# A step of 64 tokens of four batches instead of 128 tokens of two, in a kernel of linear attention followed by an MLP

## The chip, the cores and the metric

The kernel runs on one core of a Trainium2 chip. The metric is the time of one execution on the device in microseconds; before the change the median of three runs is 581.27 us (580.01 to 582.3). TensorE (PE) multiplies matrices, VectorE (DVE), ScalarE (ACT) and GpSimd (POOL) work on tiles, and SyncE (SP) issues most DMAs. Each engine works through its own queue in order and waits at semaphores.

## The reference

`r`, `k`, `v`, `w` have 4 batches, 8 heads, 768 tokens and 48 columns; `u` has one row for each head. A state of 48x48 for each batch and head decays by `w` from token to token. The result of the attention, 3072 tokens of 384 columns, goes through an MLP with 2048 hidden columns.

```
for t in range(S):
    cur = einsum('bhd,bhe->bhde', u[None] * kt, vt)
    y[:, :, t] = einsum('bhd,bhde->bhe', rt, state + cur)
    state = wt[:, :, :, None] * state + einsum('bhd,bhe->bhde', kt, vt)
x = y as (4*768, 384)
h = x @ w_in                          # 384 x 2048
g = h * erf(softplus(h))
out = g @ w_out                       # 2048 x 384
```

The two weights come as 64-bit floats, all else as 32-bit.

## The kernel before

The work is cut into 12 steps. A step takes 256 tokens: 128 tokens in a row (C) of each of two batches (NJ = 2); the two halves of 64 tokens (HC, NC = 2) are chunks that follow each other in time. Steps alternate between the two pairs of batches (`SPC` = 2), so that a pair's state passes from step s to step s + 2. Heads lie in pairs: e = 0 and 1 fill partitions 0 to 47 and 64 to 111, and JP = 8 counts batch times four pairs.

**Attention of a step.** Within a chunk the attention is made level by level: at level l TensorE multiplies left and right halves of blocks of 2^l tokens (`level_products`, L615), VectorE takes the wanted blocks into `own` (`take_level`, L633; the last level by ScalarE, L644) and scales r and k by products of decays (`scale`, L317). POOL makes these products (`totals`, L355, and L407). `from_own` (L650) multiplies `own` with v into `y`, in two halves with a `fence` (L666, a small VectorE copy) between. `through_state` (L673) adds r times the state: the state at the step's start `S` for the first chunk, `middle` for the second. `state_part` (L725) multiplies the transposed k with v for both chunks; from it come `middle` (faded start plus first part) and then `S_next` (faded `middle` plus second part): a POOL multiply into `faded`, a VectorE add, a POOL multiply, a VectorE add. After that y goes to `xT`. The last of the four groups of rows in y (`y3`) has to be shifted to other partitions: by small DMAs (L720), but in step 0 by three matmuls with a matrix of ones and zeros (`apart`, L700, in `hop`), which add into y before ScalarE copies it to xT.

**MLP.** `hidden` (L1064) multiplies xT with w_in (L1097, six matmuls for two of 16 columns of tiles, "a piece"), `project` and `project_fast` multiply with w_out (L1129, L1212). Pieces of the MLP of earlier steps stand in TensorE's queue between the levels of the present one, in an order written by hand (`place`, `beside`, `USUAL`, `LATE`). Steps 0 to 4 have a code path of their own (`attend_first`, `attend`); steps from 5 on go through `attend_late`, which makes the near levels on VectorE and POOL and takes k from a DRAM copy (`k_blocks`, `kT`, `spread_blocks`). The last two steps share their first product (`hidden_of_two`, L1300).

**Order.** The instructions of all five queues stand in the order in which the program calls them (`manual_schedule`).

**Weights.** In the first steps the 64-bit weights become 32-bit. `convert` (L222) has stages for each of 16 tiles: `l` loads the words by two DMAs of SP, behind a marker (a one-element copy, L241 or L243, that writes into the words' buffer and so makes the load wait for something), `b` scales the high words on ScalarE (L258), `r` the low words (L266), `h` shifts on VectorE (L275), `o` adds on POOL (L288). Three buffers hold words. In step 0, tiles 0 and 1 are loaded; the load of tile 2 stands behind the fence (L901), those of 3 and 4 behind the first copy into xT (L707), those of 5 and 6 behind the new state (L926). I call them load 2, load 3 and so on.

**Step 0** (`attend_first`, L819) has an inner loop over levels 2 to 5 with fillers on TensorE (`keep_busy`, a product with a zero state, L943; `stay_warm`, L934). After the last level come a filler, eight transposes of k (L889), the first `from_own`, `fence`, `state_part` of the first chunk, the second `from_own`, `middle`, `through_state` of the second chunk and `hop`. The second chunk's state part and the new state (`pending`, L921) wait for level 2 of step 1. Step 1 (`attend`, L948) puts `hop` in the middle of its level 1, and then a piece of step 0's MLP between its levels.

Of the kernel before, what the change touches and what calls it, by code (L numbers as in the profile page):

```python
# [61 lines left out]
def kernel(  # L62
# [21 lines left out]
    NB, n_pairs = out.shape[:2]  # L84
# [4 lines left out]
    SPC = NB // NJ  # L89
    assert C == P == NC * HC and HC == 1 << LOG and NE == 2 and D <= EP and NP * NE * D == DM == KT * P  # L90
    assert n_steps == SPC * n_pairs and NP == KT + 1 == 4 and NG == 2 and P // NEAR * NH == P
# [15 lines left out]

    states = [[const.tile([P, JP, D], FP32, name=f"s_{i}_{n}") for n in range(2)] for i in range(SPC)]
    middle = const.tile([P, JP, D], FP32, name="middle")
    faded = [const.tile([P, JP, D], FP32, name="faded")] * NC  # L110
# [111 lines left out]
    def convert(weights):  # L222
# [24 lines left out]
        def scale_high(i, part=slice(0, 2)):  # L247


            if i not in held:  # L250
                return
            if i < 2:
                base = ps_m.tile([P, NP * C], FP32, name="m")[:, :DM]
            else:
                base = y[:].rearrange("p e q j t -> p e (q j t)")[:, :, :DM]
            high = held[i]["words"][:, part, :, 1].bitcast(FP32)
            if i < signed:
                nc.scalar.activation(base, high, AF.Prelu, scale=2.0**-112, alpha=-(2.0**32))  # L258
            else:
                nc.scalar.mul(out=base, in_=high, mul=2.0**-112)  # L260
            held[i].setdefault("bases", []).append((base.bitcast(I32), part))
# [97 lines left out]
    def prepare(s):  # L359
# [63 lines left out]
        else:  # L423
            half = view(tots[NEAR_LOG + 1], 1, [[2, NC], [C >> NEAR_LOG + 1, JP]])
            quarter, last = (
                view(tots[NEAR_LOG], n, [[4, NC], [C >> NEAR_LOG, JP]]) for n in (1, 3)
            )
            to = over_blocks[:].rearrange("p (h b) n -> p b h n", h=NC)
            nc.gpsimd.tensor_mul(to[:, 0], quarter, half)
            nc.gpsimd.tensor_copy(out=to[:, 1], in_=half)  # L430
            nc.gpsimd.tensor_copy(out=to[:, 2], in_=last)
# [138 lines left out]
        if levels == NEAR_LOG:  # L570
            sum_up(NEAR_LOG, 0)
            sum_up(NEAR_LOG, 1)
            k_blocks = dram.tile([P, NEAR, D], FP32, name="k_blocks")
# [8 lines left out]
        if levels == NEAR_LOG:  # L582
# [16 lines left out]
    def parts_of(s):  # L599

        c, i = divmod(s, SPC)
        in_t, vt = loaded[s]
        made, tots, tot = ready[s]
        ends = tot.rearrange("p (n h) -> p n h", h=NC)
        return c, in_t, vt, made, states[i][c % 2], states[i][1 - c % 2], ends
# [67 lines left out]
    def through_state(s, xT):  # L673

        c, in_t, _, _, S, _, _ = parts_of(s)
        for h, state in enumerate((S, middle)):
            if not (c or h):
                continue
            t = slice(h * HC, (h + 1) * HC)
            for j, q in ((0, 2), (1, 2), (1, 0), (0, 0)) if not s else np.ndindex(NJ, NP // 2):  # L680
                q = q if not s else 2 * q
                for e in range(NE):
                    for p in (q + e, q + 1 - e):
# [3 lines left out]
                            lhsT=state[rows(e), n, :],  # L687
                            rhs=(in_t[:, 0, n] if s else first_pair(0, n))[rows(e), t],
# [7 lines left out]
        if not s:  # L696

            def hop():
                for kk in range(KT):
                    nc.tensor.matmul(  # L700
                        parts[kk], lhsT=apart[:, kk],
                        rhs=y3[:].rearrange("p (j t) -> p j t", j=NJ),
                        start=False, stop=True, skip_group_check=True,
                    )
                for kk in range(KT):
                    nc.scalar.copy(by_kk[kk], parts[kk])
                stages["l"](3, xT[:, KT - 1, 0:1], True)  # L707
                stages["l"](4)
                load_w(2)

# [14 lines left out]
    def state_part(s, kT, ps, halves=None):  # L725

        vt = loaded[s][1]
        if halves is None:
            halves = range(1 if s >= n_steps - SPC else NC)
        for n in range(JP):  # L730
            for h in halves:
                for e in range(NE):
                    t = slice(h * HC, (h + 1) * HC)
                    nc.tensor.matmul(  # L734
                        ps[h][e][rows(e), n, :D],
# [32 lines left out]
    def attend_late(s, run):  # L768

        c, in_t, vt, own, S, S_next, ends = parts_of(s)  # L770
# [10 lines left out]
        if before:  # L781
# [6 lines left out]
        nc.gpsimd.tensor_mul(faded[0][:], S[:], ends[:, :, 0:1].to_broadcast([P, JP, D]))  # L788
# [3 lines left out]
        kT = kTs[s]  # L792
        nc.vector.tensor_mul(
            kT[:].rearrange("p (e n) d -> p n e d", e=NE),
            kT[:].rearrange("p (e n) d -> p n e d", e=NE), spread[s][:],
        )
# [4 lines left out]
        if s + 1 < n_steps:  # L801
# [4 lines left out]
        ps = products([P, NC, JP, HC], 0)  # L806
        ps = [[ps[:, h]] * NE for h in range(NC)]
        state_part(s, kT, ps)
        run(2, following)
        nc.vector.tensor_add(middle[both], faded[0][both], ps[0][0][both, :, :D])  # L810
        run(3, following)
        if s < n_steps - SPC:
            nc.gpsimd.tensor_mul(
                faded[1][:], middle[:], ends[:, :, 1:2].to_broadcast([P, JP, D])
            )
            nc.vector.tensor_add(S_next[both], faded[1][both], ps[1][0][both, :, :D])
        run(4, following)

    def attend_first(xT):  # L819
# [5 lines left out]
        c, _, vt, made, S, S_next, ends = parts_of(0)  # L825
# [50 lines left out]
        for j, half in enumerate(halves):  # L876
            level_products(pp, first_pair, LOG, half)
            scale(0, LOG, batch=j)
        take_level(own, pp, LOG)

        kT = att.tile([P, NH, D], FP32, name="kT", bufs=1)
        kT_by_e = kT[:].rearrange("p (e n) d -> p e n d", e=NE)
        turned = [products([P, NE, JP, HC])]
        keep_busy(turned[0], (DM,))
        for j, half in enumerate(halves):
            if j:
                turned.append(products([P, NE, JP, HC]))
            for i, n in enumerate(half):
                nc.tensor.transpose(  # L889
                    turned[j][:, 0, 2 * i : 2 * i + 2], first_pair(1, n), ident[:]  # L890
                )
        from_own(0, own, 1)
        for half, ps, copy in zip(halves, turned, (nc.scalar.copy, nc.vector.tensor_copy)):
            copy(
                kT_by_e[:, :, half.start : half.stop],
                ps[:, 0].rearrange("p (n e) d -> p e n d", e=NE)[..., :D],
            )
        stages["b"](1, 0)
        stages["b"](1, 1)
# [3 lines left out]
        stages["h"](0)  # L903
        stages["h"](0)
        ps = [[products([P, NE, JP, HC], 1 - e)[:, e] for e in range(NE)]]
        state_part(0, kT, ps, (0,))
        from_own(0, own, 0)
        nc.scalar.copy(middle[rows(1)], ps[0][1][rows(1), :, :D])
        nc.vector.tensor_copy(middle[rows(0)], ps[0][0][rows(0), :, :D])
        stages["r"](1)  # L910
        stages["h"](1)
        stages["h"](1)
        wait_for(HC - 1)
        stages["o"](0)
        nc.gpsimd.tensor_mul(faded[1][:], middle[:], ends[:, :, 1:2].to_broadcast([P, JP, D]))
        totals(1)
        stages["o"](1)
        totals(*range(2, LOG + 1))
        through_state(0, xT)

        def pending():  # L921
            part = products([P, NE, JP, HC], turns["next"])[:, 0]
            state_part(0, kT, ps + [[part] * NE], (1,))
            nc.vector.tensor_add(S_next[both], faded[1][both], part[both, :, :D])
            load_third()
            stages["l"](5, S_next[:, 0, 0:1])  # L926

        turns["pending"] = pending
# [10 lines left out]
    def keep_busy(pp, columns=(DM, DM // 2)):  # L939

        zeros = states[1][0][:].rearrange("p n d -> p (n d)")
# [6 lines left out]
    def attend(s, xT, early, place, behind):  # L948

        c, in_t, vt, made, S, S_next, ends = parts_of(s)  # L950
# [718 lines left out]
```

## Time and profile before

| what | value |
|---|---|
| median of 3 runs | 581.27 us |
| profiled execution, its own time | 581.53 us |
| its span | 579.7 us |
| VectorE busy | 429.0 us |
| ScalarE busy | 354.8 us |
| POOL busy | 244.8 us |
| moved by DMA, mean over the span | 63.24 MB, 109 GB/s |
| of it, `w_in` words | 16 transfers of 384 KB, 5.3 us to landing |
| output tiles `o` | 23 transfers of 192 KB, two of 96 KB |
| a late step, from one L627 to the next | 281.87 to 326.17 us |

The profile is one execution seen by the hardware profiler; its times start at the span's start. A row of the timeline gives start and length, engine, line and operation, output and inputs, the number of instructions and, in brackets, how long the engine had been idle before and for what. TensorE shows two passes for each matmul of 32-bit numbers, so 16 matmuls are "x32". PEld is TensorE's loading of weights, PEclk its granted clock as a share of the full one. A line of the chain gives start, length and what ran.

### The profile page before, as it was taken

What the parts mean: (1) busy time and instruction counts of PE and PEld (TensorE: products, weight loads), DVE (VectorE), ACT (ScalarE), POOL (GpSimd) and SP (SyncE); (2) the same over time, 40 slices, a digit from 0 to 9 for tenths busy, and PEclk for the clock granted to TensorE, in tenths of its full rate; (3) what the DMA queues carried; (4) which work ended last, traced back from release to release, by engine and by line L of the source; (5) the groups of instructions that cost most, each with busy time, mean ns of one, the idle gap of its engine ahead of it and who ended that gap; (6) DMA issues with size and microseconds to landing.
All of it is one profiled execution on the core that took longest, in us unless ns stands there. A gap on an engine that the chain in (4) does not pass through costs nothing.

```text
span 579.7 us, 16499 instructions
## 1 busy us (share of the span) xinstructions
PE 572.8 (99%) x7240; PEld 492.2 (85%) x7240; DVE 429.0 (74%) x462; ACT 354.8 (61%) x478; POOL 244.8 (42%) x264
## 2 busy tenths in 40 slices
PE   8999999999999999999999999999999999999997
PEld 6678887688578668998998998898898899988997
DVE  7775876998894789699599599599599527256640
ACT  3658777545444698756766766766666661388700
POOL 3557391604793885284185175176174000000000
PEclk9999999999999999999999999999999999999999
DMA  7695662350453314245235236234232201000000
GB/s 261 190 325 233 235 207 83 148 161 2 145 151 98 107 44 169 41 139 177 41 125 192 39 124 193 39 111 163 47 110 83 47 8 37 1 1 2 28 27 28
DMA packets 54081, 63.24 MB, mean 109 GB/s; under 512 B 35160, under 2 KB 40568, under 8 KB 52984
## 3 DMA queue, kind: packets, MB, share of 16 engines
q1 hardware_dynamic: 53624, 61.98, 33.8%
q8 instruction: 57, 0.93, 0.7%
q10 hardware_dynamic: 384, 0.20, 0.1%
q14 instruction: 16, 0.13, 0.1%
HBM read 52.39 MB, written 8.69 MB: 105 GB/s over the span
## 4 chain that ended last, share of the span: by engine, by line
PE 95%; DVE 1%; POOL 1%; DMA 1%; issue 1%; ACT 0%; SPq 0%; DVEq 0%; POOLq 0%; ACTq 0%
PE m L1097 35%; PE m L1212 28%; PE m L1129 11%; PE pp L627 5%; PE pp L1300 4%; PE y L1300 2%; PE y L659 2%; PE y L685 2%; PE pp L734 2%; PE m L934 1%; DMA words<-in_moe_w_in 1%; PE pp L943 1%; PE pp L1010 1%; POOL tot_sb L355 0%; PE pp L1212 0%
## 5 line engine op out<-in xcount | busy, mean ns | idle before, releaser
L1097 PE MATMUL m<-xT,w_in_sb 128*128 128x256 f32 x960 | 214.8, 382 | 0.4 <-ACT h L1106 0.3
L1097 PEld LDWEIGHTS m<-xT,w_in_sb 128*128 128x128 f32 x960 | 180.1, 190 | 25.8 <-issue 0.5
L333 DVE TENSOR_TENSOR in<-in,tot_sb 128x1024 f32<-128x1024 f32 (+1 forms) x55 | 76.4, 1389 | 16.9 <-PE pp L627 15.5
L1106 ACT COPY h<-m 128x512 f32<-128x512 f32 x80 | 46.3, 579 | 59.7 <-PE m L1097 59.7
L1129 PE MATMUL m<-w_out_sb,h 128*128 128x384 f32 x192 | 64.3, 491 | 0.0
L1129 PEld LDWEIGHTS m<-w_out_sb,h 128*128 128x128 f32 x192 | 35.8, 190 | 23.4
L1212 PE MATMUL m<-mixed,h 128*128 128x192 f32 x256 | 45.6, 332 | 0.0
L1212 PE MATMUL m<-w_out_sb,h 128*128 128x192 f32 x256 | 44.8, 329 | 0.0
L1212 PEld LDWEIGHTS m<-mixed,h 128*128 128x128 f32 x256 | 41.4, 190 | 0.9
L1057 ACT ACT_TABLE_LOAD x30 | 38.5, 1283 | 5.9 <-DVE h L1062 5.4
L1212 PEld LDWEIGHTS m<-w_out_sb,h 128*128 128x128 f32 x256 | 41.6, 190 | 0.3
L1212 PE MATMUL m<-w_out_sb,room 128*128 128x192 f32 x240 | 41.5, 326 | 0.0
L1053 ACT ACT_TABLE_LOAD x30 | 38.5, 1283 | 3.2 <-issue 2.7
L462 POOL TENSOR_TENSOR words<-words,own 128x384 f32<-128x384 f32 x21 | 30.7, 1462 | 22.8 <-DVE words L493 13.1
L627 PEld LDWEIGHTS pp<-in 48*48 48x48 f32 (+4 forms) x2368 | 30.1, 120 | 11.8 <-issue 6.2
L503 POOL TENSOR_TENSOR words<-words 128x384 f32<-128x384 f32 x28 | 39.7, 1447 | 0.0
L1212 PEld LDWEIGHTS m<-w_out_sb,room 128*128 128x128 f32 x240 | 39.4, 190 | 0.0
L455 POOL TENSOR_TENSOR own<-rest 128x384 f32<-128x384 f32 x7 | 9.8, 1396 | 60.8 <-ACT o L1218 49.8
L627 PE MATMUL pp<-in 48*48 48x32 f32 (+4 forms) x2368 | 34.0, 206 | 0.2 <-DVE in L333 0.2
L503 POOL TENSOR_TENSOR rk<-words 128x384 f32<-128x384 f32 x28 | 32.4, 1186 | 0.0
L528 DVE TENSOR_REDUCE sums<-rk 128x16 f32<-128x768 f32 (+2 forms) x31 | 31.6, 1021 | 0.0
L1053 ACT ACTIVATE room<-h 128x1024 f32<-128x1024 f32 x28 | 29.6, 1057 | 0.3
(204 smaller groups left out, 980.0 us busy)
## 6 DMA issues: line engine op xcount, KB each, us to landing
in<-in_rkw SPq DMA_DIRECT2D x8, 1024.0 KB, 5.1
words<-in_moe_w_in SPq DMA_DIRECT2D x16, 384.0 KB, 5.3
words<-in_moe_w_out SPq DMA_DIRECT2D x16, 384.0 KB, 5.5
words<-in_rk_rows SPq DMA_DIRECT2D x8, 768.0 KB, 5.7
w<-in_rkw SPq DMA_DIRECT2D x11, 512.0 KB
v<-in_v SPq DMA_DIRECT2D x12, 384.0 KB, 5.5
out<-o SPq DMA_DIRECT2D x23, 192.0 KB, 3.1
in<-in_rkw SPq DMA_DIRECT2D x7, 512.0 KB, 6.0
```

What stands on the lines that cost most here:

```text
L333: nc.vector.tensor_mul(halves, halves, view(tots[level - 1], 0, [[1, n], [2, nb], [0, half]]))
L462: engine.tensor_mul(to, to, of[:, :, None, :].to_broadcast([P, NEAR // 2 // half, half, D]))
L503: engine.tensor_mul(to[:, i], r[:, half:], k[:, part * rows + i, None].to_broadcast([P, half, D]),)
L528: nc.vector.tensor_reduce(out=to, in_=of, axis=mybir.AxisListType.X, op=ALU.add)
L627: nc.tensor.matmul(to, lhsT=rk(1, n)[rows(e), s0 : s0 + m], rhs=right, start=True, stop=True,)
L1053: nc.scalar.activation(sp_room, chunks[0], AF.Softplus)
L1057: nc.scalar.activation(at, sp_room, AF.Erf)
L1097: nc.tensor.matmul(ps[:, ff, :], lhsT=w_in_sb[:, g * FG + f + ff, kk * P : (kk + 1) * P], rhs=xT[:, kk, :], start=kk == 0, stop=kk == KT - 1,)
L1106: nc.scalar.copy(h[:, f : f + FT, :], ps[:])
L1129: nc.tensor.matmul(ps[j][:], lhsT=gs[g][:, f, j * C : (j + 1) * C], rhs=w_out_sb[:, g * FG + f, :], start=g + f == 0, stop=g == NG - 1 and ...
L1212: nc.tensor.matmul(to, lhsT=a[:, f], rhs=b[:, f], start=start and f == 0, stop=f == FG - 1, skip_group_check=True,)
L1300: nc.tensor.matmul(to[:, e], lhsT=a[:, 2 * i + e], rhs=b, start=start and not k, stop=True, skip_group_check=True,)
```

## The change

A step takes 64 tokens of all four batches: what was the chunk (NC = 2) is now a second pair of batches. The two parts of a step are independent in time, there is one state for all four batches, and it passes from step to step.

- States: two tiles of 128x768 in place of five of 128x384. `middle` goes. One POOL multiply fades the state (`fade_state`) and one VectorE instruction makes the next (`next_state`). The state that `through_state` reads is ready from the step before.
- Step 0 starts from no state and has no `through_state` products. Step 11 needs no next state: no `state_part`, `fade_state`, scaling of kT, `k_blocks` or, in step 10, `spread_blocks` for it.
- Step 0's end is put together anew: no filler and no transposes after the last level; four ScalarE copies in place of two take it into `own`; r is not scaled at the last level, and k by one VectorE instruction after the fence; the second weight tile's high words go through a products bank. A part of step 1's level 1 is put ahead of `from_own`.
- `hop`: the three matmuls with `apart` write PSUM buffers of their own while ScalarE copies y to xT, and three VectorE adds bring them into xT. It is called before step 1's levels, not within its level 1.
- Transposes and the kT copy of step 0 come after step 1's level 2 (`turn`), with the load of tile 5 behind the kT copy, the whole `state_part` of step 0 after level 3 (`to_state`).
- An output tile holds 64 tokens of two batches, so it is stored by two DMAs (`write_out`), in step 11 the last tile by four.
- The host lays out its arrays to match; their shapes in DRAM stay.

```diff
@@ states
-    states = [[const.tile([P, JP, D], FP32, name=f"s_{i}_{n}") for n in range(2)] for i in range(SPC)]
-    middle = const.tile([P, JP, D], FP32, name="middle")
-    faded = [const.tile([P, JP, D], FP32, name="faded")] * NC
+    states = [const.tile([P, NC, JP, D], FP32, name=f"s_{n}") for n in range(2)]
+    faded = const.tile([P, NC, JP, D], FP32, name="faded")
@@ scale_high
-            if i < 2:
+            if not i:
                 base = ps_m.tile([P, NP * C], FP32, name="m")[:, :DM]
+            elif i == 1:
+                base = products([P, NE, NP * C], turns["next"])[:, part, :DM]
@@ new functions
+    def fade_state(s):
+        nc.gpsimd.tensor_mul(
+            faded[:], states[s % 2][:],
+            view(ready[s][2], 0, [[1, NC], [NC, JP], [0, D]]),
+        )
+    def next_state(s, ps):
+        got = ps[both].rearrange("p h n t -> p h n t")[..., :D]
+        if s:
+            nc.vector.tensor_add(states[1 - s % 2][both], faded[both], got)
+        else:
+            nc.vector.tensor_copy(out=states[1][both], in_=got)
+    def write_out(s, j, o, part=slice(None)):
+        for h in range(NC):
+            nc.sync.dma_start(
+                out=out[s, j * NC + h, :, part], in_=o[h * HC : (h + 1) * HC, part]
+            )
@@ through_state
-        for h, state in enumerate((S, middle)):
-            if not (c or h):
-                continue
+        for h in range(NC) if s else ():
...
-                            lhsT=state[rows(e), n, :],
-                            rhs=(in_t[:, 0, n] if s else first_pair(0, n))[rows(e), t],
+                            lhsT=S[rows(e), h, n, :],
+                            rhs=in_t[rows(e), 0, n, t],
@@ hop
-                for kk in range(KT):
+                def shift(kk):
+                    ps = ps_m.tile([P, NJ, C], FP32, name="m")
                     nc.tensor.matmul(
-                        parts[kk], lhsT=apart[:, kk],
+                        ps[:], lhsT=apart[:, kk],
                         rhs=y3[:].rearrange("p (j t) -> p j t", j=NJ),
-                        start=False, stop=True, skip_group_check=True,
+                        start=True, stop=True,
                     )
+                    return ps
+                shifted = [shift(kk) for kk in range(2)]
                 for kk in range(KT):
                     nc.scalar.copy(by_kk[kk], parts[kk])
                 stages["l"](3, xT[:, KT - 1, 0:1], True)
                 stages["l"](4)
                 load_w(2)
+                for kk in range(KT):
+                    if kk == 2:
+                        shifted.append(shift(kk))
+                    nc.vector.tensor_add(by_kk[kk], by_kk[kk], shifted[kk][:])
@@ attend_late
-        nc.vector.tensor_add(middle[both], faded[0][both], ps[0][0][both, :, :D])
+        if not last:
+            next_state(s, ps)
         run(3, following)
-        if s < n_steps - SPC:
-            nc.gpsimd.tensor_mul(
-                faded[1][:], middle[:], ends[:, :, 1:2].to_broadcast([P, JP, D])
-            )
-            nc.vector.tensor_add(S_next[both], faded[1][both], ps[1][0][both, :, :D])
@@ attend_first, behind the products of the last level
+        turns["pp"] = products([P, NE, JP, HC])
+        second = by_pair(ready[1][0])
+        level_products(turns["pp"], second, 1, range(3))
+        for swap in (1, 0):
+            for h in range(NC):
+                some, e = slice(h * HC, h * HC + half), h ^ swap
+                nc.scalar.copy(of[some, e, :, half:], got[some, e, :, :half])
+        stages["h"](0)
+        stages["h"](0)
         from_own(0, own, 1)
         fence()
         stages["l"](2, seen[:, 0:1])
         load_v(1)
+        stages["o"](0)
+        stages["b"](1, 0)
+        stages["b"](1, 1)
         from_own(0, own, 0)
+        nc.vector.tensor_mul(
+            view_k, view_k, view(tot, 1, [[NP * C >> LOG - 1, NJ], [2, NP * NC], [0, HC // 2]])
+        )
         stages["h"](1)
         stages["h"](1)
         totals(1)
+        through_state(0, xT)
+        level_products(turns["pp"], second, 1, range(3, JP))
+        turns.pop("hop")()
+        stages["r"](1)
         stages["o"](1)
         totals(*range(2, LOG + 1))
+        kT = att.tile([P, NH, D], FP32, name="kT", bufs=1)
+        def turn():
+            ps = products([P, JP, P], turns["next"])
+            for n in range(JP):
+                nc.tensor.transpose(ps[:, n, :], first_pair(1, n), ident[:])
+            nc.scalar.copy(
+                kT[:].rearrange("p (e n) d -> p e n d", e=NE),
+                ps[:].rearrange("p n (e d) -> p e n d", e=NE)[..., :D],
+            )
             load_third()
-            stages["l"](5, S_next[:, 0, 0:1])
+            stages["l"](5, kT[:, 0, 0:1])
+        def to_state():
+            ps = products([P, NC, JP, HC], turns["next"])
+            state_part(0, kT, ps)
+            next_state(0, ps)
-        turns["pending"] = pending
+        turns["pending"] = {2: turn, 3: to_state}
```

## The prediction

> **What bounds the kernel now.** I read the page first, for the engine that sets the end.
>
> ```profile
> PE 572.8 (99%) x7240; PEld 492.2 (85%) x7240; DVE 429.0 (74%) x462; ACT 354.8 (61%) x478; POOL 244.8 (42%) x264
> ...
> PE 95%; DVE 1%; POOL 1%; DMA 1%; issue 1%; ACT 0%; SPq 0%; DVEq 0%; POOLq 0%; ACTq 0%
> ```
>
> TensorE (PE) is busy for 99% of the span and makes 95% of the chain that ended last. A change pays only where TensorE's queue gets shorter or waits less. The chain in order of time shows where it is not pure TensorE: before 43.5 us, where VectorE, POOL and, longest, a weight load (5.64 us) come between.
>
> ```profile
> 34.76 5.64 DMA words<-in_moe_w_in
> ...
> 57.73 0.59 PE y L685 x32
> ...
> 90.56 1.04 PE y L685 x64
> ...
> 392.57 0.86 PE pp L734 x64
> ...
> 436.88 0.85 PE pp L734 x32
> ...
> 480.91 0.81 PE pp L734 x30
> ```
>
> After 43.53 us it is nearly all TensorE. The other rows show prices: half of `state_part` (x32) takes as long as all of it (x64), and half of `through_state` 0.59 us against 1.04. Then the timeline of the opening, for when each thing happens.
>
> ```profile
> 27.93 2.86 PE L1097 MATMUL m<-xT,w_in_sb 128*128 128x256 f32 x12
> ...
> 28.55 2.99 SPq L150 DMA_DIRECT2D words<-in_moe_w_in  x4
> ...
> 34.38 2.91 SPq L150 DMA_DIRECT2D words<-in_moe_w_in  x4
> ```
>
> The MLP of step 0 starts at 27.93 us (L1097), weight loads 3 and 4 leave SP at 28.55, 5 and 6 at 34.38. Busy time by stretch (20 to 25, 25 to 30, 35 to 43 us) shows room in the DMA early and none late (0.37, 0.60, 0.99):
>
> ```profile
> 20.00:25.00 5.00, 4.41 (x149) 3.48 (x151) 4.11 (x10) 3.37 (x7) 1.86 (x3) 1.00 0.37 110
> 25.00:30.00 5.00, 4.74 (x83) 3.87 (x74) 2.02 (x2) 3.29 (x8) 5.00 (x5) 1.00 0.60 185
> ...
> 35.00:43.00 8.00, 7.70 (x154) 6.29 (x152) 6.43 (x7) 6.13 (x10) 5.04 (x4) 1.00 0.99 374
> ```
>
> **The opening, part by part.** Out of TensorE's queue before the MLP go the filler (0.91), the transposes (1.01, done later at the same price), `through_state` of step 0 (about 1.0, L685 from 23.96) and one of two half `state_part`s (0.9); the other becomes a whole one later. I lay the new queue order on the old durations, from the last level's products (end 19.45, unchanged). The four copies into `own` take 0.37 each (ScalarE's 128x256 row, 25.36) and end at 20.0, 20.4, 20.8 and 21.15; 24 passes of step 1's level 1 cover TensorE to 20.1. First `from_own` 20.5 to 21.15 (0.65), `fence` 0.18 to 21.35, second to 22.05, rest of level 1 to 22.75. ScalarE scales weights (2 x 0.53) to 22.2 and copies y3 (0.37) to 22.6, so the shifts (0.52 each, six passes of L700 in 1.56) run from 22.8. The xT copies end at 23.5, the marker (0.19) sends loads 3 and 4 at 23.75. VectorE comes from the fence, one scaling of K (0.65, half of L326's two in 1.28) and two weight shifts (0.5 each), free at 23.3. Its three adds are new: 0.42 each, between the 128x192 add (0.35) and the 128x384 add (0.56) from PSUM. The third shift waits for the first add (23.8) to free its buffer and ends at 24.4; the last add ends at 24.9, its operand is wanted at 25.3. The MLP starts at 24.4: 3.5 us earlier.
>
> Some of that lead is spent again. Queue, with the chain's durations: MLP piece 2.79 (x12), level 2 1.05, transposes 1.05, piece 2.79, to 32.1. Level 3 then writes the bank of the transposes and so waits for ScalarE's kT copy, queued behind the conversion of weight load 3; that is the new wait, and behind it stand level 3, `state_part` and the next piece. Load 3: load 2 leaves after the fence at 21.65, the first bytes come about 2.45 later (the fastest landing, 3.5, less 0.39 MB at 374 GB/s, 1.05), a whole load takes 2.1, v's 1.05 between: 21.65 + 2.45 + 2.1 + 1.05 + 2.1 = 29.4. Then L258 0.88, L266 0.91, h copy 0.58, kT copy 0.80: 32.6, so TensorE waits 0.5. Level 3 and `state_part` end at 34.55. POOL's marker for load 5 waits for kT and holds back `o(2)` behind it: 32.6 + 0.4 + 1.82 = 34.85, another 0.3 of waiting. Piece, level 4, piece: 41.5. Load 5 leaves at 32.9, with loads 4 and w_2 just landed, so 4.55 later is 37.4; L258, VectorE's shift (0.96) and scaling (1.21) make 40.6 < 41.5. Level 5 starts at 41.5 instead of 43.53: **-2.0 us**. With none of these waits it is 24.4 + 2.79 x 4 + 1.05 x 4 + 0.9 = 40.65: -2.9, the one bound. The other bound is from the weight loads' own row (fastest, median, slowest):
>
> ```profile
> DMA to landing us min/median/max: 3.5/5.6/8.4
> ```
>
> With 8.4 for loads 3 and 5, load 3 lands at 32.15, kT is copied at 35.3, load 5 leaves at 35.55 and lands at 43.95, level 5 at 47.1: +3.5. I take -2.0, since load 2 comes in the same emptiness as before.
>
> [...] Here the granted clock is 1.00 in every stretch of the opening though 0.59 of 5 us is idle at 20 to 25. [...]
>
> **After the opening.** Step 1 runs all of `through_state`, 1.04 for 0.59: **+0.45**. Step 10's `state_part` is whole for the price of a half (0.86 for 0.85), step 11's goes: 481.77 - 480.91 = **-0.85**. Step 10 no longer spreads blocks for step 11: from level 6 to the next products 0.94 (430.54 to 431.48) becomes 0.69 (474.83 to 475.52): **-0.25**. Each output tile leaves in two transfers. In mid-run SP issues 23 more at 0.34; the work that hides it is loads issued 20 us ahead of use. At the end nothing does: the last add ends at 577.07 and one more issue follows, **+0.35** (0.33 to 0.38 by SP's rows).
>
> ```profile
> 576.72 0.35 DVE L1244 TENSOR_TENSOR o<-o,pp 128x192 f32<-128x192 f32 x1 [1.73 <-PE pp L1212]
> ```
>
> At nothing I cost: the state update, one POOL multiply of 128x768 for two of 128x384 (1.66 by 0.83 each, at most 3.64 by the 1.82 of L915) and one VectorE add of about 0.92 for two of 0.54. In the steady steps POOL idles 12.45 us after the first fade, and the state is wanted a step later. In step 1 cover is thinner: a fade of 3.64 would let VectorE scale step 2 only 0.5 before TensorE asks; at most 0.5 if that is gone. The first memset of a state grows from 0.42 to about 0.8 ahead of the identity; TensorE waits 0.65 for data at 7.09 anyway.
>
> Sum: -2.0 + 0.45 - 0.85 - 0.25 + 0.35 = -2.3. The profiled execution took 581.53 (span 579.7 and 1.8 around it) and would take 579.2; it stands 0.26 above the median of the runs, 581.27, from which I get **579.0**.
>
> **The rivals.** *The lead survives whole.* Load 3 lands before 28.9, or `o(2)` is early, and TensorE never waits: -2.9 for -2.0, 578.1. For it: DMA is 0.37 and 0.60 busy where the loads now go. Against it: the kT copy stands in ScalarE's line behind load 3, and POOL behind it.
>
> *The transfers set the opening.* TensorE comes early but load 5 lands when it did, level 5 starts at 43.5, the lead is gone: -0.3, 581.0. For it: load 5 is in the chain with 5.64 us, and the DMA is 0.99 busy then. Against it: load 5 leaves 1.5 us sooner and 1.57 MB are through before it.
>
> *The weight loads get slow, and the line kT, POOL, load 5 carries it on* (the slower side). Priced above at 8.4 us each: +3.5 - 0.3 = +3.2, 584.5. It costs from the point where load 5 lands later than 40.5, which is 7.6 after its issue. For it: one load did take 8.4. Against it: that one was issued at 38.5 into the 0.99 stretch, these into an emptier one.
>
> That the change does not do what it says I exclude: the step order shows the counts above.
>
> **How the numbers follow.** Forecast (-0.3 to -0.5%) 0.48; whole lead 0.24; transfers 0.19; slow loads 0.09. What a measurement of this kernel tells from no change is about 0.5%, 2.9 us: 578.4 and 584.2. The whole lead is past it by 0.3, so two thirds of its chance and a third of the forecast's give faster 0.32; slow loads, past the other bound by 0.3, give slower 0.08; the rest is 0.60. The range runs from the whole lead less 1.1 (the spread of the runs is +-0.2%) to the transfers plus 1.0: 577.0 to 582.0.
>
> **What would show it.** In the changed profile: first L1113 matmul at 24.4; third load issued near 23.75 and kT copied near 32.6; a wait of TensorE before level 3 on ScalarE and one on POOL before the third piece, under 1 us together; level 5 at 41.5; from there every step at the old length, the last state product gone; the last store issued 0.35 later. Wrong is the forecast if level 5 starts outside 40.6 to 43, or if a steady step is not the 44.3 us of now (326.17 less 281.87).

## The result, and the profile after

The changed kernel takes 586.18 us (median of 4 runs, 584.95 to 586.79) against 581.78 us (4 runs) for the kernel before on the same chip: a ratio of 1.0078, 95% interval 1.005 to 1.0107. Measured again later it was 585.52 us and 1.0083 (1.0057 to 1.0108). It is slower, by 0.8%; the forecast was 579.0 us, range 577.0 to 582.0.

The page of the changed kernel, the two lines that were shown of before:

```profile
PE 571.0 (98%) x7234; PEld 489.5 (84%) x7234; DVE 433.7 (74%) x451; ACT 354.6 (61%) x478; POOL 251.6 (43%) x247
...
PE 60%; ACT 3%; DVE 1%; ACTq 0%; issue 0%
```

TensorE has 1.8 us less to do, and the span still grew by 4.6: it stands idle 6.4 us longer. (This page's chain could be followed back only to 195.67 us, so its 60% don't compare with the 95% of before.) Where the time went is read by setting the start of the same TensorE instruction beside its start before the change:

| TensorE instruction | before | after | after less before | by the forecast |
|---|---|---|---|---|
| level 5 of step 1 | 43.53 | 42.27 | -1.26 | -2.0 |
| level 2 of step 3 | 97.83 | 98.43 | +0.60 | -1.55 |
| level 6 of step 3 | 123.16 | 125.02 | +1.86 | -1.55 |
| first `from_own` of step 5 | 237.09 | 241.23 | +4.14 | -1.55 |
| first `from_own` of step 10 | 458.57 | 462.48 | +3.91 | -1.80 |
| second `from_own` of step 11 | 484.94 | 488.13 | +3.19 | -2.65 |
| end of the span | 579.7 | 584.3 | +4.6 | -2.3 |

So four places lost: steps 1 and 2 (1.86, of which 0.45 was forecast), step 3 (1.26), step 5 (2.28) and the end (1.4). The steady steps are 44.30 us as before, and steps 10 and 11 gave 0.23 and 0.7. The opening, from the timeline of the changed kernel:

```profile
21.29 0.33 PE L681 MATMUL y<-own,v 64*48 64x64 f32 x8 [0.37 <-DVE seen L690]
22.15 0.55 PE L681 MATMUL y<-own,v 64*48 64x64 f32 x23 [0.54 <-issue]
...
25.03 2.82 PE L1113 MATMUL m<-xT,w_in_sb 128*128 128x256 f32 x12
...
33.60 1.08 PE L649 MATMUL pp<-in 48*60 48x32 f32 x64 [0.77 <-ACT kT L942]
...
35.73 2.86 PE L1113 MATMUL m<-xT,w_in_sb 128*128 128x256 f32 x12 [0.32 <-POOL w_in_sb L288]
...
42.27 0.92 PE L649 MATMUL pp<-in 48*48 48x32 f32 x64
...
24.21 2.45 SPq L148 DMA_DIRECT2D words<-in_moe_w_in  x4
```

The two waits that were forecast are there (0.77 for kT, 0.32 for POOL; 0.5 and 0.3 were said). What was not: a wait of 0.54 us inside the second `from_own`, for "issue", that is for nothing the profile shows. Step 5, the largest loss, in the changed kernel:

```profile
219.95 4.86 DVE L333 TENSOR_TENSOR in<-in,tot_sb 128x1024 f32<-128x1024 f32 x2
224.74 1.21 DVE L1204 TENSOR_TENSOR room<-h,y 128x1024 f32<-128x1024 f32 x1
...
218.30 3.45 POOL L1168 TENSOR_TENSOR w_out_sb<-w_out_sb 128x1536 f32<-128x1536 f32 x1
221.72 2.02 POOL L407 TENSOR_TENSOR tot_sb<-w 128x512 f32<-128x512 f32 x1
...
225.98 1.02 ACT L1185 COPY y<-h 128x1024 f32<-128x1024 f32 x1 [3.44 <-DVE room L1204]
226.93 0.58 ACT L1122 COPY h<-m 128x512 f32<-128x512 f32 x1
...
227.56 4.62 PE L1113 MATMUL m<-xT,w_in_sb 128*128 128x256 f32 x19 [1.66 <-ACT h L1122]
```

and in the kernel before:

```profile
218.19 2.48 DVE L333 TENSOR_TENSOR in<-in,tot_sb 128x1024 f32<-128x1024 f32 x2
...
222.35 0.83 POOL L813 TENSOR_TENSOR faded<-middle,tot_sb 128x384 f32<-128x384 f32 x1 [5.03 <-DVE middle L810]
223.14 3.46 POOL L1153 TENSOR_TENSOR w_out_sb<-w_out_sb 128x1536 f32<-128x1536 f32 x1
```

Before, POOL stood 5.03 us at its second fade, waiting for `middle`, and only then mixed the weights (once in the program, in step 5). The change takes that fade away, POOL mixes 5 us earlier, beside VectorE's two scalings (L333), and these take 4.86 for 2.48. (In the changed kernel POOL's next instruction, L407, runs beside the second of them too; the reverse experiment below tells the two apart.) Behind them the blend (L1204) is late, behind that ScalarE's copy (L1185), behind that in ScalarE's line an `h` copy, and TensorE waits 1.66 us for it at 227.56.

### The profile page after: what moved, and what is told of

The parts are those of the page before. It is cut to its first block, busy times and chain, and to the rows that moved or that the text cites. A ratio compares the mean times of both kernels' runs of the same rounds, so it can differ in the third digit from the quotient of the medians.

```text
span 584.3 us, 16488 instructions
## 1 busy us (share of the span) xinstructions
PE 571.0 (98%) x7234; PEld 489.5 (84%) x7234; DVE 433.7 (74%) x451; ACT 354.6 (61%) x478; POOL 251.6 (43%) x247
## 4 chain that ended last, share of the span: by engine, by line
PE 60%; ACT 3%; DVE 1%; ACTq 0%; issue 0%
PE m L1226 28%; PE m L1113 20%; PE pp L1314 4%; PE y L1314 2%; PE pp L649 1%; PE y L681 1%; PE y L704 1%; ACT L1073 1%; DVE in L333 1%; ACT L1069 1%; PE pp L759 1%; ACT room L1069 1%; PE pp L1226 0%; ACTq L747 0%; ACT pp L1073 0%
## 5 line engine op out<-in xcount | busy, mean ns | idle before, releaser
L333 DVE TENSOR_TENSOR in<-in,tot_sb 128x1024 f32<-128x1024 f32 (+1 forms) x55 | 81.3, 1479 | 17.7 <-PE pp L649 17.3
L407 POOL TENSOR_TENSOR tot_sb<-tot_sb 128x256 f32<-128x256 f32 (+4 forms) x50 | 30.1, 602 | 3.8
```

What stands on the lines that cost most here:

```text
L333: nc.vector.tensor_mul(halves, halves, view(tots[level - 1], 0, [[1, n], [2, nb], [0, half]]))
```

## The experiments

**POOL held back in step 5.** Edit, behind stage 3 of `attend_late`:

```diff
         run(3, following)
+        if s == DIRECT + 1:
+            nc.gpsimd.tensor_copy(
+                out=faded[both, 0, 0, 0:1], in_=states[1 - s % 2][both, 0, 0, 0:1]
+            )
```

> Changed kernel, but in step 5 POOL makes a one-column copy out of the new state into faded before it mixes the weights, so that it stands still until VectorE's state add, as it did before the change for middle. Theory (the merged state update set POOL free, and its weight mix and totals ran beside VectorE's two L333 and slowed them): the two L333 at 220 us fall from 4.86 to about 2.5 us, the wait of 1.66 us of TensorE at 227.6 goes, and the time falls by about 2.3 us from 586.2 to 583.9; the rest of the profile is unmoved. Rival (the wait comes from ScalarE's line, which is 1.9 us late in this step anyway, or the mix held back is wanted soon): L333 gets short but TensorE waits elsewhere, the time stays at 586.2 or more.

Measured: 584.25 us (12 runs), 1.006 (1.0037 to 1.0082) of before. Timeline of this kernel:

```profile
217.93 2.49 DVE L333 TENSOR_TENSOR in<-in,tot_sb 128x1024 f32<-128x1024 f32 x2
...
222.47 0.19 POOL L842 COPY faded<-s 112x1 f32<-112x1 f32 x1 [5.94 <-DVE s L618]
222.61 3.47 POOL L1172 TENSOR_TENSOR w_out_sb<-w_out_sb 128x1536 f32<-128x1536 f32 x1
```

A wait of 5.94 us put back on POOL makes the scalings short again. From level 6 of step 3 to the `from_own` of step 5, this kernel gains 0.16 on the one before where the changed one loses 2.28. The theory holds in its place. The gain of the median is 1.9 (1.3 against the 585.52 of the second measurement), less than the 2.4 of the profile: in 7 of the 12 executions the mean granted clock was 0.993 to 0.996, and the other five have a median of 583.02. The filler's runs below bear on this.

**The reverse, in the kernel before.** The mix goes ahead of the second fade:

```diff
-            "S2 S3 H k12y S4 H F", "s H ep m H H F G s H H H ep",
+            "S2 S3 H k12y S4 H F G", "s H ep m H H F s H H H ep",
```

> The kernel before the change, with POOL's weight mix of step 5 put ahead of its second fade, so that it no longer stands behind the wait for middle. Theory (that wait kept POOL away from VectorE): the two L333 at 218 us take 4 us or more in place of 2.48, TensorE waits 1 to 2 us for ScalarE's h copy near 226 us, and the span gets 1 to 2 us longer from there on. Rival (step 5 is lost elsewhere, such as by the one large state add): L333 slower, but no wait of TensorE and no loss.

```profile
216.13 5.55 DVE L333 TENSOR_TENSOR in<-in,tot_sb 128x1024 f32<-128x1024 f32 x2
...
215.89 3.44 POOL L1153 TENSOR_TENSOR w_out_sb<-w_out_sb 128x1536 f32<-128x1536 f32 x1
...
224.43 7.91 PE L1097 MATMUL m<-xT,w_in_sb 128*128 128x256 f32 x33 [1.77 <-ACT h L1106]
```

The same loss, in a kernel without the new states: 2.40 us from level 6 of step 5 to its `from_own` (from -1.40 to +1.00 against before). The one execution took 582.53 us; the kernel before had a median of 581.35 on that chip. The totals come at 224.26 here, after the scalings, so the mix alone does it.

**The fade of step 3 at the step's start.**

```diff
+        if s == DIRECT - 1:
+            fade_state(s)
...
-        fade_state(s)
+        if s != DIRECT - 1:
+            fade_state(s)
         next(following, None)
         place(LOG)
```

> Changed kernel, but in step 3 the fade of the state stands at the step's start, where POOL idles for 13 us, in place of after the kT copy. Theory (the fade, twice as long as before the change, slows VectorE's L535 beside it, and so the scaling that TensorE waits for): L535 falls from 2.24 us to about 1.0 to 1.6, the waits of TensorE on L333 in step 3 (0.65 and 0.49 us) shrink by 0.6 us or more, the time falls by 0.5 to 1.1 us to 585.1 to 585.7. Rival (step 3 is late because ScalarE's weight scaling L260 starts 1.2 us late behind its own transfers): L535 is shorter, but TensorE's waits in step 3 stay above 0.9 us together, and the time at 586.2.

The changed kernel, then this one (timeline):

```profile
112.28 2.24 DVE L535 TENSOR_TENSOR rk<-words,u_row 128x768 f32<-128x768 f32 x1
...
111.90 1.80 POOL L609 TENSOR_TENSOR faded<-s,tot_sb 128x768 f32<-128x768 f32 x1
...
125.02 0.76 PE L649 MATMUL pp<-in 48*32 48x32 f32 x64 [0.49 <-DVE in L333]
```

```profile
111.92 1.00 DVE L535 TENSOR_TENSOR rk<-words,u_row 128x768 f32<-128x768 f32 x1
...
23.39 0.71 PE L681 MATMUL y<-own,v 64*48 64x64 f32 x23 [1.85 <-issue]
```

(The last line is of its opening.) L535 is back at 1.00, there is no wait on L333 in step 3, and the step loses 0.18 in place of 1.26: right in its place. But the median, 585.05 us (9 runs, 1.0067, 1.0044 to 1.0091), hardly shows it, and the profiled execution took 586.57: its opening was 1.7 us worse than that of the changed kernel. Its busy time by stretch shows why (the last three numbers are the granted clock, the DMA share and GB/s):

```profile
24.00:26.00 2.00, 2.00 (x47) 1.79 (x42) 0.00 (x0) 1.80 (x6) 0.46 (x1) 0.50 1.00 373
```

Behind a wait of 1.85 us for "issue", TensorE ran at half its clock.

**An output tile by one DMA.**

```diff
-        for h in range(NC):
-            nc.sync.dma_start(
-                out=out[s, j * NC + h, :, part], in_=o[h * HC : (h + 1) * HC, part]
-            )
+        nc.sync.dma_start(out=out[s, j * NC : (j + 1) * NC, :, part], in_=o[:, part])
```

> Changed kernel, but an output tile leaves by one DMA over both batches, as before the change. Theory (the end is longer because SP issues six transfers of the last tiles one after the other): from the last add's end to the span's end 2.7 us in place of 4.03, the time falls by 1.3 us to 584.9, nothing moves before 575 us. Rival (the landing of the last bytes is longer because a tile's rows go to two batches): the end stays at 4.0 us, the time at 586.2.

A miss on both theories: 590.86 us (5 runs, 1.0156, 1.0133 to 1.018). From the last add to the end it is 9.7 us. Stretch of this kernel behind the last add (same columns):

```profile
583.00:585.00 2.00, 0.00 (x0) 0.00 (x0) 0.00 (x0) 0.00 (x0) 0.00 (x0) 0.50 0.14 46
```

The DMA share is 0.14 of 16 engines, as much as 2.2 of them busy all the time (an estimate from this row); in the changed kernel it is 0.29 in the 3.03 us behind the last add (580.27 to 583.30). Why the share of one DMA over two batches is so low was not shown. By the two ends, 9.7 us and 4.03, this layout of steps is better stored by two DMAs of 64 rows.

**All three together.**

> All three edits together: POOL held in step 5, one DMA for an output tile, the fade of step 3 at the step's start. If the three causes are independent, the gains add up: 586.2 - 2.3 - 1.3 - 0.8 = 581.8, within 0.5% of the kernel before (581.8). If one wait only takes the place of another, less: 583 or more.

588.31 us (6 runs): the store spoils it (9.6 us behind the last add). The other two add up: from level 2 of step 3 to the first `from_own` of step 5 the changed kernel takes 142.80 us and this one 139.08, which is 3.72 less, where the hold alone gives 2.59 and the early fade alone 1.09.

**The kernel before with two stores for each tile.** Each `dma_start` of an output tile becomes two, of rows 0 to 63 and 64 to 127.

> The kernel before the change, with each output tile stored by two DMAs of 64 rows and nothing else changed. Theory: from the last add's end to the span's end 4.0 us in place of 2.67, and no other step moves by more than 0.3 us. Rival (the stores in mid-run cost too, in SP's line ahead of the loads): the steps from 6 on get longer than 44.30 us.

```profile
575.48 3.67 SPq L610 DMA_DIRECT2D out<-o  x6
...
577.44 0.35 DVE L1249 TENSOR_TENSOR o<-o,pp 128x192 f32<-128x192 f32 x1 [1.73 <-PE pp L1217]
```

The add ends at 577.79, the span at 581.5: 3.7 us in place of 2.67 (4.0 expected), 1.0 of the 1.36 that the changed kernel lost there (580.27 to 584.3, 4.03). Steps from 6 on stay 44.30. Steps 1 and 2 take 0.55 longer than in the profile before, and step 3 0.47, more than the 0.3 allowed. The stores can't be the cause of the first, since the first of them leaves at 115.35 us: this much the kernel before varies by itself. Its one execution took 583.31 us.

**Two queues for the last stores** (with the hold and the early fade).

```diff
+            queue = nc.scalar if h and s == n_steps - 1 else nc.sync
-            nc.sync.dma_start(
+            queue.dma_start(
```

> Changed kernel with POOL held in step 5, the fade of step 3 at the step's start, and in the last step the second store of each tile from ScalarE's queue in place of SP's. Theory (six issues in a row on one queue make the end longer): from the last add's end to the span's end about 2.9 us in place of 4.1; with the 580.1 us span of the kernel with POOL held, less 1.1 of step 3 and 1.2 here, the span is 577.8 and the time about 579.6 in executions whose mean granted clock is 0.998 or more, and some 3.5 us more in those at 0.993 to 0.996, which come too (median 580 to 582). Rival (the last bytes, not the issue, set the end): the end stays at 4 us, 580.8.

583.49 us (12 runs, 1.003, 1.0014 to 1.0046). The end takes 3.37 us (575.98 and 0.35, to 579.7): 0.7 gained of 1.2 expected. Issuing on one queue is about half of the 1.36; what the rest is was not tried.

**A filler in the opening** (besides these three edits).

```diff
         stages["b"](1, 1)
+        stay_warm(2)
         from_own(0, own, 0)
```

> The kernel before it in this list, with two 256-column matmuls (1.1 us) of filler put into TensorE's queue between the fence of step 0 and the second from_own, where TensorE waits 0.4 us for VectorE and then 0.3 to 1.85 us for something the profile names only issue. Theory (the granted clock falls to 0.5 at 23.5 us in some executions because TensorE is nearly idle from 21 to 23 us since the change): no execution below 0.997, the times fall together to a band of 2.5 us, the median is lower than without the filler by 0.5 to 2 us, though the filler itself may cost up to 0.7. The wait named issue ends 2.4 us after the instruction packet at 19 to 20.75 us as before it, and four matmul passes earlier in the order (x4 in place of x8), since it stands at a fixed count of TensorE's instructions. Rival (the clock falls for another reason, later): still executions at 0.993 to 0.996, and the median as without or 0.5 more.

581.13 us (12 runs, 0.9998, 0.9983 to 1.0013), 2.4 below the kernel without it on the same chip (0.5 to 2 were expected). All 12 executions had a mean clock of 0.999 or more; without it 5 of 12 were at 0.993 or 0.994. The theory holds on the clock. But the clock is not all of the 2.4: the 7 executions without the filler at 0.997 or more have a median of 582.56, still 1.4 above, and what gave that is open. The wait for "issue" was not in this profile; the filler ends at 21.4, when such a wait would have ended too.

**The changed kernel again, and with the filler alone.**

> The changed kernel itself, for the clock of its executions. Theory (what cuts the granted clock in the opening comes with the change, and hits some executions): some of them have a mean clock of 0.993 to 0.996 and are about 3 us longer than those at 0.998 or more; the median of the latter is 585 to 586. Rival (the clock fell in the experiments for what they add): all at 0.997 or more, one band.

> The changed kernel with the 1.1 us of filler between the fence and the second from_own of step 0 as its only edit. Theory (the filler keeps TensorE from the idle stretch at 21 to 23 us): all executions at 0.997 or more, in one band, and the median about 584, 2 us below that of the changed kernel; the losses of step 3 (1.2), step 5 (2.3) and the end (1.4) stay. Rival: executions at 0.993 to 0.996 still come, or the median is that of the changed kernel.

Again: 585.52 us, six executions, three at 0.995 or 0.996. So the clock does fall in the changed kernel itself; but those three took 585.3, 585.7 and 588.16 and the two at 1.0 585.33 and 587.0, so a cost of 3 us in each such execution is not borne out. Filler alone: 585.1 us (6 runs, 1.0063, 1.004 to 1.0087), not told apart from the changed kernel, a miss. Five of the six executions had a mean clock of 1.0; the profiled one, at 0.996, shows the wait at another place:

```profile
18.65 0.24 PE L649 MATMUL pp<-in 48*32 48x32 f32 x2
20.20 0.74 PE L649 MATMUL pp<-in 48*32 48x32 f32 x62 [1.31 <-issue]
```

**POOL held and the filler.**

> The changed kernel with POOL held in step 5 and the filler of step 0, and nothing else. Of the filler two measurements disagree: 2.4 us gained on top of the other edits, 0.4 alone. Theory (the filler keeps the clock at full speed, and pays where nothing later hides the opening): all executions at 0.997 or more and a median of 582 to 583, against 584.25 with POOL held alone. Rival (the filler is worth little, and the 2.4 came from chance in the opening): executions at 0.993 to 0.996 still come, or the median is 583.8 or more.

583.02 us (12 runs, 1.0028, 1.0014 to 1.0043), 1.2 less than with POOL held alone (measured on another chip). This is nearer to the theory, but between the two: one execution of 12 was at 0.996, the others at 0.998 or more, and the median is just past the 583 said. Those 11 have a median of 582.93, and with POOL held alone the five at 0.998 or more had 583.02: here the clock is all that the filler gave. Over the kernels with POOL held and two-part stores, 12 of 24 executions without the filler were at 0.996 or less, and 2 of 36 with it.

**kT ahead of weight load 3** (with all edits above).

```diff
+                send("br")
...
-        (("", "br"),) * 2 + (("", "brl"),) * 3 + (("", "l"), ("", ""), ("", ""), ("", "brl")),
+        (("", ""), ("", "br")) + (("", "brl"),) * 3 + (("", "l"), ("", ""), ("", ""), ("", "brl")),
```

> The kernel with POOL held, the fade of step 3 early, the last stores on two queues and the filler, and besides ScalarE's kT copy of step 0 ahead of the conversion of weight load 3. Theory (in the opening TensorE waits 0.59 us for that copy and 0.33 for POOL's add, which stands behind the copy's marker): kT is copied at about 30 us in place of 31.9, the two waits go, level 5 of step 1 starts at about 40.5 us in place of 41.45, and the median is 580.2 in place of 581.1. Rival (the conversion of load 3, now 0.8 later, is wanted as soon): the wait moves to the third piece or to level 4, and the time stays.

kT is copied at 30.35, both waits go, one of 0.31 for VectorE comes at 34.23. From level 2 to level 5 of step 1 takes 13.54 us for 14.08, but the time, 581.73 us (12 runs, 1.0, 0.9981 to 1.0019), isn't told apart from 581.13: this profile has "issue" waits of 0.42 at 22.11 and 0.79 at 46.66. No version tried beats the kernel before; two equal it.

**Three stretches in all profiles.** A single profile could mislead, so here is the length of three stretches in us, from start to start, in every profile of the record.

| from, to | kernel before | code of the change | with the edit for this place |
|---|---|---|---|
| level 5 of step 1, level 2 of step 3 | 54.30, 54.30, 54.85 | 55.18 to 56.87 (11 profiles) | none tried |
| level 2 to level 6 of step 3 | 25.31, 25.33, 25.80 | 25.70 to 26.59 (6) | fade early: 25.31 (4), 25.51 |
| level 6 of step 3, first `from_own` of step 5 | 113.77, 113.93; mix first 116.32 | 116.19 to 116.22 (5) | POOL held: 113.76 to 113.77 (6) |

The loss of step 5 is the same in every profile, and goes in every one that holds POOL. That of step 3 varies from 0.4 to 1.3 us, though L535 takes 2.23 or 2.24 us in all six.

## Why the prediction was wrong, point by point

**The step that failed** is "At nothing I cost: the state update". Its cover, "in the steady steps POOL idles 12.45 us after the first fade, and the state is wanted a step later", was right for the two instructions and for the steady steps, which stayed at 44.30. It was wrong for step 5, which is no steady step (it has the mix), and it asked only what the new instructions cost, not what POOL does with the time it no longer waits. The removed wait had kept POOL off VectorE: 2.28 us, shown in both directions. In step 3 the one fade of 768 in place of 384 beside VectorE's L535 cost 1.26 in the changed kernel's profile and 0.4 to 1.3 in the six with the fade there, against 0.0 to 0.2 when moved. The price was in the profile before, where L534 took 1.58 beside the small fade and its like 0.95; one of the three profiles of the kernel before loses 0.5 there as well. The prediction named two signs of being wrong, level 5 outside 40.6 to 43 and a steady step that is not 44.3 us; neither came, since no sign looked at the steps that are not steady.

**The last store, +0.35**, was mis-sized: +1.36. One more issue was counted where three more stand on SP's queue (six rows in 3.67 us), and each of the six took 0.47 to 0.60 us where the three of before took 0.33 to 0.39. Two queues got back 0.7 of it.

**The opening, -2.0**, had its mechanism right: the MLP starts at 25.03 (24.4 said, 27.93 before), both waits came, and level 5 is at 42.27 (41.5 said). The size, -1.26, is short of the forecast, and the term left out is the wait for "issue": 0.54 in this profile, 1.83 when measured again. With POOL held and with the filler level 5 stands at 41.55 and 41.45, but this is not all gain: the first level products of step 0 start at 6.62 and 6.54 there, at 7.09 in the kernel before and 7.11 in the changed one. From those products on, level 5 comes 36.4 us later in the profile that the prediction used, 35.2 in the changed kernel and 34.9 in these two. Two experiments leave the opening of the kernel before as it was, and there it is 35.6 (mix first) and 36.8 (two stores); the changed kernel measured again, with its 1.83 us wait, took 36.5. So the gain of the opening is 1.5 us at best against the profile before, it varies by more than 1 us from one execution to the next, and one profile of each kernel does not fix it.

**The clock.** The prediction's sum has no term for it: the granted clock was 1.00 in every stretch of the opening before, and the longest wait that I had worked out was 0.5 us. The waits were longer: 0.77 for kT, and up to 1.83 for "issue". In the four executions of the result the mean clock was 0.997 to 1.0, so the clock is not what made 586.18. But measured again, the changed kernel shows:

```profile
24.10 0.55 PE L681 MATMUL y<-own,v 64*48 64x64 f32 x23 [1.83 <-issue]
...
26.00:27.00 1.00, 1.00 (x4) 0.46 (x3) 0.42 (x1) 1.00 (x3) 0.00 (x0) 0.50 0.95 356
```

What is missing from 1.00 in such stretches, doubled and summed, says how long the half speed lasts: 3.4 us here (clocks of 0.62, 0.50, 0.50 and 0.67 from 25 to 29 us), and 3.4 with the early fade and with the filler alone too. Ahead of it, measured again, TensorE was busy 0.77, 0.63, 0.26 and 0.00 of the four us from 20 to 24. With the filler alone it was busy 0.90, 0.00 and 0.80 of the three us from 18 to 21, with one wait of 1.31 us, and the clock was 0.50 in each us from 21 to 24. In the changed kernel's first profile it was busy 0.86, 0.33, 0.85 and 1.00 of the four us from 20 to 24, with its wait of 0.54, and the clock was 1.00 in each. How long a wait it takes to lower the clock was not tried. The kernel before stayed at 0.999 or more in all 20 executions of the first series; in the three later ones, 57 executions, it was at 0.994 in two and at 0.997 in two. So the change makes the low clock frequent, but it isn't new with the change. Half speed for 3.4 us is 1.7 us of TensorE's full-speed time (an estimate from the rows above), and how much of it reaches the changed kernel's median stays open.

**Steps 1 and 2** lost 1.4 beyond the +0.45 of `through_state`. The profile shows waits of 0.45 (a transfer of xT), 0.16 (L333) and 0.30 (h copy). It was 0.4 to 2.1 in the other ten profiles with the same code there (55.18 to 56.87 us in the table above, less 54.30 and 0.45), and nothing was tried on it. With POOL held, the fade early, two queues and the filler it is the largest loss that is left, and its cause is open.

**Right** were +0.45 for `through_state` (-1.12 to -0.67 in step 1), -0.25 (measured -0.23) and -0.85 (-0.7), and the length of the steady steps.

**The rivals.** None named the mechanism. The one on the slower side gave 584.5, near the time, by late weight loads; level 5 was early, so its number was nearly met by something else, which is chance.

## What to carry to other kernels

A wait that a change removes from an engine off the critical path is an event to price like an added instruction: ask what that engine starts earlier and what runs beside it then. One step in twelve that does something special is where to look, not the steady step. Filler on TensorE can also be what keeps its clock up: with POOL held, 12 of 24 executions without it were at 0.996 or less, and 2 of 36 with it. Count it as cover before taking it out. It did not cover the wait for "issue" reliably: one of four profiles with the filler is free of it. And look for issues in a row on one queue at the very end.

## What the runs showed of the hardware

**VectorE and POOL in each other's way: in these pairs who starts first keeps its time.** In the kernel before, L333 (128x1024) took 1.21 to 1.23 us with POOL idle, and L288 1.81 with VectorE idle (83.68). In step 2 of the kernel before, VectorE began 0.11 us ahead and POOL paid; in the one with the filler POOL began 0.07 ahead and VectorE paid:

```profile
68.67 1.23 DVE L333 TENSOR_TENSOR in<-in,tot_sb 128x1024 f32<-128x1024 f32 x1
...
68.78 2.81 POOL L288 TENSOR_TENSOR w_out_sb<-w_out_sb,rest 128x768 int32<-128x768 int32 x1 [1.57 <-DVE w_out_sb L280]
```

```profile
67.66 2.85 DVE L333 TENSOR_TENSOR in<-in,tot_sb 128x1024 f32<-128x1024 f32 x1 [0.21 <-PE pp L650]
...
67.59 1.83 POOL L288 TENSOR_TENSOR w_out_sb<-w_out_sb,rest 128x768 int32<-128x768 int32 x1 [1.58 <-DVE w_out_sb L280]
```

**TensorE's "issue" wait stands at a fixed place in its queue:** between the 8th and 9th pass of the second `from_own`, or 126 passes earlier (behind two passes of level 6, as above); with the filler's four passes ahead it moved to behind the third. A pass is a weight load and a matmul (7234 of each in the changed kernel), so 126 passes are 252 instructions; the trace of the kernel with all three edits, which has both waits (0.21 us at 18.34, 0.38 at 21.65), shows three semaphore instructions of TensorE between them, 255 in all. The changed kernel measured again and the kernel with kT ahead each have a second such wait further on, at 49.26 and 46.66: from the first to the second it is 509 passes and 6 semaphore instructions in both, 1024 instructions. The wait ends 2.1 to 2.6 us after a packet of the DMA queue named "instruction", here in the quarter microsecond from 19.00 with POOL held:

```profile
q8 instruction: 1, 0.02, 23.7%
```

TensorE went on at 21.40. With the packet in the quarter from 19.75 it went on at 22.15, from 20.75 at 23.39, from 21.5 at 24.10. That TensorE waits for what the packet brings is my reading of these times; no view names it. In the opening the waits were 0.21 to 1.85 us long. The kernel before can have such a wait too: 0.48 us at 27.54 in the run with two stores. Why the packet comes later in some executions (19.2 to 21.7 us in the profiles with the wait inside the second `from_own`) was not tried.
